# Five small edits to a fused attention and feed-forward kernel: a second load queue, a second buffer, a later transpose, another group order, smaller last stores

## The chip, the cores and the metric

The kernel runs on one core of one Trainium2 chip. The metric is device time in microseconds (us) of one execution. Before the change it was 820.72 us, the median of 3 runs (819.7 to 821.32). TensorE is written PE, VectorE DVE, ScalarE ACT, SyncE SP. A "q" after an engine's name means its sequencer issuing a DMA.

## The reference, cut to what matters

```python
# q, k, v: (8 batches, 8 heads, 576 tokens, 64); g_norm: (64,)
kv  = np.einsum('bhsd,bhse->bhde', k, v)
o   = np.einsum('bhsd,bhde->bhse', q, kv)
rms = np.sqrt(np.mean(o * o, axis=-1, keepdims=True) + 1e-06)
x   = (o / rms * g_norm)                  # then laid out as 4608 tokens x 512
a, b = x @ w1, x @ w2                     # 512 x 1024 each
out = ((a * b) @ w3) @ w_out              # 1024 x 1024, 1024 x 512
```

The four weights come as 64-bit floats, the rest in fp32.

## The kernel before

The 4608 tokens are worked on as 9 groups of 512. Each batch has 576 tokens, so 8 groups are the first 512 tokens of a batch, and the ninth, the *leftover group*, holds the last 64 tokens of all eight. The product w3·w_out is computed once, at the start (the *fold*), in 8 *chunks* of 128 columns of w3 and 128 rows of w_out. Each chunk is loaded as 64-bit words, converted to fp32 by two ACT and four DVE steps, transposed on PE and multiplied. PE's order is written by hand, and at the start that of ACT, DVE and SP too.

The loads of a chunk: the first one (i = 0) in four loads of 256 KB, the others in two of 512 KB, all from SP's queue. The first is converted in three pieces.

```python
src = w3[0:DF // 2, i * P:(i + 1) * P].rearrange("(m p) f -> p m f", p=P)
cols = w_out[i * P:(i + 1) * P, :].rearrange("p (c f) -> p c f", c=1)
n = 1 if i else 2
for h in range(n):
    load(slice(h * 512 // n, (h + 1) * 512 // n), src[:, h * 4 // n:(h + 1) * 4 // n, :])
for h in range(n):
    f = slice(h * DM // n, (h + 1) * DM // n)
    load(slice(512 + f.start, 512 + f.stop), cols[:, :, f])
# ... cut ...
cuts = [0, 1024] if i else [0, 256, 512, 1024]
```

The setup fills the four load buffers and then loads the norm's gain, 64 numbers, twice into a column of 128 partitions, from ACT's queue:

```python
for _ in range(RAW):                      # RAW = 4
    load_next()
nc.scalar.activation(const.tile([P, 1], FP32, name="warm"), eps_col, AF.Sqrt)
g_src = g_norm.rearrange("(d o) -> d o", o=1)
for e in range(2):
    nc.scalar.dma_start(out=g_col[e * D:(e + 1) * D, :], in_=g_src)
keep_warm(14)                             # filler matmuls
begin_next(); end_next()                  # convert chunk 0
turn_w3(0, 0)                             # transpose its w3 half
keep_warm(5)
# ... cut: for each chunk c: convert c + 1, multiply c, transpose c + 1 ...
```

The norm: ACT squares a bank of PSUM, DVE sums per head, with one buffer for the squares.

```python
for i in range(n):
    sq = work.tile([P, G], FP32, name="sq", bufs=1)[:, 0:w]
    nc.scalar.activation(sq, o_ps[i], AF.Square)
    nc.vector.tensor_reduce(out=inv[:, i], in_=sq.rearrange(...), axis=AX.X, op=ALU.add)
```

The attention of the next batch is cut into pieces, which run between the products of the present group. Every second batch also transposes the leftover tokens' q (`q_t_left`):

```python
pieces = [[(begin, 0, 1)], [(middle, 0)], [(turn, 0), (turn, 1)],
          [(begin, 2, 3)], [(middle, 1)], [(turn, 2), (turn, 3)], [], []]
if b % 2:
    pieces[0].append((q_t_left,))
```

The groups run in the order 0 to 8, the leftover group last; its results go out in eight stores of 128 KB from SP's queue:

```python
for m in range(2):
    for l in range(2):
        b = 2 * (2 * half + m) + l
        nc.sync.dma_start(out=out[b * S + G:(b + 1) * S, :],
                          in_=o_sbs[half][l * L:(l + 1) * L, m, :])
```

## Time and profile before

| of the profiled run, span 817.5 us | us |
|---|---|
| PE busy | 803.4 |
| PE waits for the identity matrix, at the start | 1.9 |
| PE waits for conversions at the start, two waits | 3.8 |
| PE waits at the leftover q's transposes | 1.1 |
| PE waits for normalised rows | 1.0 |
| from PE's last matmul to the end | 5.9 |

PE is busy for 98% of the span, so the time is PE's own work plus what PE waits for. Everything else matters only where it makes PE wait, at the start and at the end. The lines behind this table are in the prediction. Two further lines of before also belong here, and the prediction does not show them. The first is in the list of waits, on the row of PE's weight loads (columns: what waited, for what, us in total, times, longest); the second is in the full list of DMA issues (KB each, us from issue to landing).

```profile
PEld at L302 <- ACT kv_sb L284: 2.3, 4, 1.2
```

```profile
g_col<-in_g_norm_dram ACTq DMA_DIRECT2D x2, 0.2 KB, 3.8
```

The weight loads that feed PE waited 2.3 us in four places where the matmul row shows 1.1 us in two. And a load of 0.2 KB took 3.8 us to land.

### The profile page before, as it was taken

To read this page: it belongs to the slowest core of one execution; us is meant where nothing else is said; L and a number is where in the kernel's file an instruction comes from. 1 tells how busy PE (TensorE), PEld (TensorE's weight loads), DVE (VectorE), ACT (ScalarE), POOL (GpSimd) and SP (SyncE) were. 2 spreads that over 40 slices of the span, in tenths; PEclk is the share of its full clock that TensorE was granted. 3 is DMA by queue.
4 is the path that set the end of the run, shared out by engine and by line. 5 is a ranking of instruction groups with operands and counts; after the bars stand their busy time and mean duration, and the time that the engine had idled before them with its cause. 6 is when DMAs were issued, how large, how long until landed. Compare 5 with 4: busy or idle time off the path is not lost.

```text
span 817.5 us, 12566 instructions
## 1 busy us (share of the span) xinstructions
PE 803.4 (98%) x5334; PEld 675.4 (83%) x5334; DVE 364.7 (45%) x680; ACT 267.8 (33%) x499; POOL 1.8 (0%) x8
## 2 busy tenths in 40 slices
PE   7999999999999999999999999999999999999997
PEld 4455788888888888888888888888888888888886
DVE  6967997315521553155315531543154414512521
ACT  6677643234312331243123322331233212212210
POOL 0000000000000000000000000000000000000000
PEclk9999999999999999999999999999999999999999
DMA  9996434032103210312032202120210010001002
GB/s 315 331 334 173 147 91 91 1 128 62 32 1 128 71 36 1 105 58 57 1 104 71 59 1 85 61 76 1 89 41 1 1 52 1 0 1 52 1 0 52
DMA packets 60152, 59.53 MB, mean 73 GB/s; under 512 B 15425, under 2 KB 56385, under 8 KB 60097
## 3 DMA queue, kind: packets, MB, share of 16 engines
q1 hardware_dynamic: 59936, 58.73, 23.8%
q8 instruction: 42, 0.69, 0.4%
q14 instruction: 14, 0.11, 0.0%
q10 hardware_dynamic: 160, 0.00, 0.0%
HBM read 49.28 MB, written 9.44 MB: 72 GB/s over the span
## 4 chain that ended last, share of the span: by engine, by line
PE 93%; DVE 3%; ACT 1%; DMA 1%; issue 1%; SPq 0%; DVEq 0%; ACTq 0%
PE mm L470 78%; PE mm L455 5%; PE at L273 2%; PE at L343 2%; PE at L376 2%; PE at L292 2%; DMA raw<-in_moe_w_out_dram 1%; PE at L442 1%; DVE ab L149 1%; ACT kv_sb L284 0%; DVE w_sb L159 0%; DVE inv L312 0%; PE at L302 0%; PE at L361 0%; DVE w_sb L153 0%
## 5 line engine op out<-in xcount | busy, mean ns | idle before, releaser
L470 PE MATMUL mm<-xT,w_sb 128*128 128x256 f32 x768 | 176.2, 379 | 0.0
L470 PEld LDWEIGHTS mm<-xT,w_sb 128*128 128x128 f32 x768 | 145.9, 190 | 20.3 <-issue 0.5
L470 PE MATMUL mm<-xc,ws 128*128 128x256 f32 x576 | 130.2, 379 | 0.0
L470 PEld LDWEIGHTS mm<-xc,ws 128*128 128x128 f32 x576 | 109.4, 190 | 14.9
L483 ACT COPY u<-mm 128x512 f32<-128x512 f32 x90 | 52.7, 586 | 195.1 <-PE mm L470 194.4
L470 PE MATMUL mm<-w3o_sb,ab 128*128 128x256 f32 x432 | 96.2, 379 | 0.0
L596 DVE TENSOR_TENSOR c<-mm,u 128x512 f32<-128x512 f32 x36 | 24.9, 690 | 157.9 <-PE mm L470 157.7
L483 ACT COPY p<-mm 128x512 f32<-128x512 f32 x90 | 52.8, 586 | 129.8 <-PE mm L470 129.5
L470 PEld LDWEIGHTS mm<-w3o_sb,ab 128*128 128x128 f32 x432 | 82.1, 190 | 11.2
L470 PE MATMUL mm<-xc,w_sb 128*128 128x256 f32 x288 | 68.8, 382 | 0.0
L470 PE MATMUL mm<-raw 128*128 128x256 f32 x288 | 63.6, 379 | 0.0
L455 PE MATMUL mm<-chunks,ab 128*128 128x512 f32 x128 | 60.0, 601 | 1.9 <-DVE chunks L159 1.9
L470 PE MATMUL mm<-xT,ws 128*128 128x256 f32 x256 | 61.6, 383 | 0.0
L470 PEld LDWEIGHTS mm<-raw 128*128 128x128 f32 x288 | 54.7, 190 | 7.4
L470 PEld LDWEIGHTS mm<-xc,w_sb 128*128 128x128 f32 x288 | 52.8, 190 | 6.7
L312 DVE TENSOR_REDUCE inv<-sq 128x8 f32<-128x512 f32 (+1 forms) x40 | 25.2, 629 | 61.5 <-ACT sq L311 61.5
L470 PEld LDWEIGHTS mm<-xT,ws 128*128 128x128 f32 x256 | 46.7, 190 | 6.0
L625 DVE TENSOR_TENSOR raw<-mm,u 128x512 f32<-128x512 f32 x9 | 6.2, 692 | 97.0 <-PE mm L470 97.0
L597 DVE TENSOR_TENSOR ab<-c 128x256 f32<-128x256 f32 x108 | 45.7, 423 | 2.8
L455 PEld LDWEIGHTS mm<-chunks,ab 128*128 128x128 f32 x128 | 21.9, 190 | 23.5 <-issue 17.9
L596 DVE TENSOR_TENSOR c<-p,u 128x512 f32<-128x512 f32 x36 | 24.8, 689 | 27.3 <-ACT u L483 27.3
L311 ACT ACTIVATE sq<-at 128x512 f32<-128x512 f32 (+1 forms) x40 | 22.2, 555 | 41.1 <-PE at L343 21.7
(83 smaller groups left out, 779.2 us busy)
## 6 DMA issues: line engine op xcount, KB each, us to landing
raw<-in_moe_w_dram SPq DMA_DIRECT2D x31, 512.0 KB, 7.3
k_sb<-in_k_dram SPq DMA_DIRECT2D x32, 256.0 KB, 4.5
v_sb<-in_v_dram SPq DMA_DIRECT2D x32, 256.0 KB, 4.8
q_sb<-in_q_dram SPq DMA_DIRECT2D x32, 256.0 KB, 4.9
out_dram<-raw SPq DMA_DIRECT2D x16, 512.0 KB, 2.6
raw<-in_moe_w_out_dram SPq DMA_DIRECT2D x7, 512.0 KB, 8.2
kl_sb<-in_k_dram SPq DMA_DIRECT2D x8, 128.0 KB, 5.8
vl_sb<-in_v_dram SPq DMA_DIRECT2D x8, 128.0 KB, 5.5
```

What stands on the lines that cost most here:

```text
L149: nc.vector.scalar_tensor_tensor(out=low_bits, in0=hi, scalar=0x80000000, in1=low_bits, op0=ALU.bitwise_and, op1=ALU.bitwise_or,)
L273: nc.tensor.matmul(kv_ps[e * D:(e + 1) * D, r - rs[0], :], lhsT=k_sb[:, e, cols] if j < J else kl[:, 2 * r + e, :], rhs=v_sb[:, e, cols] i ...
L292: nc.tensor.transpose(qt_ps[:, e, i, :], q_sb[:, e, i * P:(i + 1) * P], ident)
L311: nc.scalar.activation(sq, o_ps[i], AF.Square)
L312: nc.vector.tensor_reduce(out=inv[:, i], in_=sq.rearrange("p (h d) -> p h d", d=D), axis=AX.X, op=ALU.add)
L343: nc.tensor.matmul(o_ps[l][tokens, n * D:(n + 1) * D], lhsT=qT[r][rows, e, i, tokens], rhs=kv_b[rows, e, r, :], start=True, stop=True,)
L376: nc.tensor.transpose(t_ps[:, j, :], st[r // 2][:, j // 2, j % 2, m:m + 2, :], ident)
L455: nc.tensor.matmul(sums_ps[half][m], lhsT=w3T[half, c][:, m, :], rhs=chunks[:, c, 1, :], start=(c == 0), stop=(c == KF - 1),)
L470: nc.tensor.matmul(ps[:, u, :], lhsT=lhsT(a_name, u, c), rhs=rhs(b_name, c),  start=(u == 0 and c == 0 and to is None), stop=(c == chunks ...
L483: nc.scalar.copy(t, ps)
L596: nc.vector.tensor_add(c, one, two)
L597: nc.vector.tensor_mul(dst, c[:, 0, :], c[:, 1, :])
```

## The change

The intent is to shorten the waits of the table. The first chunk is loaded from two queues and converted in parts of 512 columns; the squares get two buffers; the leftover q is transposed two pieces later; the leftover group becomes the last but one; and the last group is stored block by block.

```diff
-            n = 1 if i else 2
-            for h in range(n):
-                load(slice(h * 512 // n, (h + 1) * 512 // n), src[:, h * 4 // n:(h + 1) * 4 // n, :])
-            for h in range(n):
+            queues = (nc.sync,) if i else (nc.sync, nc.scalar)
+            n = len(queues)
+            for h, queue in enumerate(queues):
+                load(
+                    slice(h * 512 // n, (h + 1) * 512 // n),
+                    src[:, h * NH // n:(h + 1) * NH // n, :], queue,
+                )
+            for h, queue in enumerate(queues):
                 f = slice(h * DM // n, (h + 1) * DM // n)
-                load(slice(512 + f.start, 512 + f.stop), cols[:, :, f])
+                load(slice(512 + f.start, 512 + f.stop), cols[:, :, f], queue)
...
-        cuts = [0, 1024] if i else [0, 256, 512, 1024]
+        cuts = [0, 1024] if i else [0, 512, 1024]
...
-                sq = work.tile([P, G], FP32, name="sq", bufs=1)[:, 0:w]
+                sq = work.tile([P, G], FP32, name="sq")[:, 0:w]
...
-            pieces[0].append((q_t_left,))
+            pieces[2].insert(0, (q_t_left,))
...
+            if last:
+                rows = out[T * S:T * S + G, j * N:(j + 1) * N].rearrange("(p j) f -> p j f", j=J)
+                parts = ((0, 1), (1, 2)) if two is None else ((0, 2),)
+                for a, b in parts:
+                    if two is None:
+                        nc.scalar.copy(dst[:, a:b], one[:, a:b])
+                    else:
+                        nc.vector.tensor_add(dst, one, two)
+                    queue = nc.scalar if a else nc.sync
+                    queue.dma_start(out=rows[:, 2 * half + a:2 * half + b, :], in_=dst[:, a:b])
+                return
...
-    for T in range(NG):
-        pieces = iter(attention(T + 1) if T + 1 < B else [])
+    groups = [*range(B - 1), B, B - 1]
+    for n, T in enumerate(groups):
+        pieces = iter(attention(T + 1) if n + 2 < NG else [])
```

More of the change, by code (lines that the diff above doesn't have):

```diff
@@ L61 @@
     KF = DF // P
+    NH = KF // 2
     J = 4
@@ L179, in load_next, with load @@
         raw = raw_tile()
-        def load(where, src):
-            nc.sync.dma_start(out=raw[:, where].rearrange("p (c m) -> p c m", c=src.shape[1]), in_=src)
+        def load(where, src, queue=nc.sync):
+            queue.dma_start(out=raw[:, where].rearrange("p (c m) -> p c m", c=src.shape[1]), in_=src)
         if what == "w":
@@ L432, in attention @@
         return [steps(fs) for fs in pieces]
-    NH = KF // 2
     w3T = {}
@@ L603, in gates, with project @@
         )
-    def project(T, between=lambda: None):
+    def project(T, between=lambda: None, last=False):
         def store(half):
@@ L732 @@
                 run(sum_ab(p))
-        if T and T + 1 < NG:
-            run(combine_x(T + 1))
-        project(T, between if T == 0 else lambda: None)
+        last = n + 1 == NG
+        if T and not last:
+            run(combine_x(groups[n + 1]))
+        project(T, between if T == 0 else lambda: None, last)
         if T == 0:
```

## The prediction

> **What bounds the kernel now.** I read the page's totals first, to learn which engine leaves no room.
>
> ```profile
> span 817.5 us, 12566 instructions
> PE 803.4 (98%) x5334; PEld 675.4 (83%) x5334; DVE 364.7 (45%) x680; ACT 267.8 (33%) x499; POOL 1.8 (0%) x8
> ```
>
> TensorE (PE) is busy for 803.4 of 817.5 us, and the change removes none of its useful matmuls. So the whole prize lies in the 817.5 - 803.4 = 14.1 us in which PE stands still, plus such filler as stands in for waiting at the start. Next I asked what PE waited for (columns: engine and line, what ended the wait, us in total, times, longest).
>
> ```profile
> PE mm L254 <- POOL ident masks.py:199: 1.9, 1, 1.9
> PE mm L455 <- DVE chunks L159: 1.9, 1, 1.9
> PE at L442 <- DVE chunks L159: 1.9, 1, 1.9
> PE at L302 <- ACT kv_sb L284: 1.1, 2, 0.9
> PE at L376 <- DVE xn L321: 1.0, 4, 0.3
> ```
>
> These sum to 7.8 us. Another 5.9 us is the tail: the timeline shows PE's last matmul ending at 811.6. That leaves about 0.4 us of crumbs. The first wait, for the identity matrix, is untouched. The change aims at the other four and at the tail, so its ceiling is about 1.9 + 1.9 + 1.1 + 1.0 + 5.9 = 11.8 us, 1.4% of the time.
>
> For the start I followed the chain that ended last, in order of time (start, duration, what; links of 0.02 us left out).
>
> ```profile
> 3.36 6.68 DMA raw<-in_moe_w_out_dram
> ...
> 10.13 1.14 ACT ab L146
> ...
> 11.29 1.23 DVE ab L149
> 12.52 0.61 DVE chunks L153
> ...
> 13.15 0.70 DVE chunks L156
> ...
> 13.88 1.24 DVE chunks L159
> ...
> 15.16 0.66 PE at L442 x4
> 15.82 3.52 PE mm L455 x8
> ```
>
> From 15.16 on PE has no gap up to 48: a chunk takes it 3.52 + 0.44 = 3.96 us, and VectorE (DVE) converts one in 3.72 (its L159 steps start at 13.88, 17.61, 21.33). So what matters is when the conversion of the *second* chunk ends, at 15.11; all later work slides with it. That conversion starts when the second chunk's w_out lands, 6.68 us after its issue. The traffic of those microseconds, by windows (last two columns: share of the DMA engines' time, GB/s):
>
> ```profile
> 3.50:4.00 0.50, 0.50 (x4) 0.50 (x4) 0.00 (x0) 0.35 (x2) 0.00 (x0) 1.00 0.68 215
> 4.00:4.50 0.50, 0.50 (x5) 0.50 (x4) 0.38 (x2) 0.50 (x3) 0.00 (x0) 1.00 0.32 82
> 4.50:5.00 0.50, 0.50 (x4) 0.50 (x4) 0.47 (x3) 0.50 (x2) 0.00 (x0) 1.00 0.65 205
> 5.00:5.50 0.50, 0.50 (x5) 0.50 (x4) 0.47 (x3) 0.09 (x1) 0.00 (x0) 1.00 0.82 291
> ...
> 9.00:10.00 1.00, 0.00 (x0) 0.00 (x0) 0.93 (x3) 0.12 (x1) 0.00 (x0) 1.00 1.05 379
> ```
>
> There is a hole between 3.5 and 5.5 us: the first 512 KB of w3 is done and w_out, issued from 1.74 on, has barely begun. Afterwards the engines are full at about 380 GB/s.
>
> **What the Trainium skill says.** "DMA: Bandwidth & Descriptors", section "Issuing engines are not separate DMA queues": DMAs of all issuing engines share the same 16 DMA engines, and issuing from several saves only sequencer time. The trace agrees as far as it goes: six loads stand one after another in SyncE's queue from 0.74 to 3.8, about 0.5 us each, and once the engines are full no second queue could add anything. So I credit the second queue with the hole and the issue time, not with bandwidth. "Perfetto Trace Analysis", section "Optimization Strategy", says that repeating gaps on the engine that should be saturated can mean too few SBUF or PSUM buffers; the waits at L302 and L376 fit that (below). "DMA: Bandwidth & Descriptors", section "Anatomy of one DMA — SWDGE (gpsimd) path", puts a fixed cost of about 2.0 us on a DMA, mostly the write receipt; it speaks of the GpSimd path, but the small output stores here, on the SyncE queue, took 2.2 to 2.4 us to land. So the tail keeps that part whatever is done.
>
> **The change, part by part.**
>
> *First chunk from two queues, in parts of 512.* The four 256 KB loads of chunk 0 are issued two and two, so chunk 1's loads are issued two places earlier on SyncE: 2 x 0.55 = 1.1 us. Bytes decide how much of that arrives. Between 3.5 and 5.5 the engines moved (215 + 82 + 205 + 291) x 0.5 = 397 KB; at some 330 GB/s (the rate of the 3.0 to 3.5 window) they would have moved 660 KB. The missing 263 KB, at 380 GB/s, is 0.7 us. So chunk 1 lands 0.7 to 1.1 us earlier, at about 9.1. Its own conversion chain (5.0 us from landing to end) is unchanged. DVE must be free for it: chunk 0 now takes two conversions of 512 columns. The w3 half lands at about 4.0 in one piece; 0.67 + 0.69 + 0.42 + 0.43 + 0.69 (the 512-column durations of before) ends it near 7.0, about as the two 256-column conversions do (6.86). The w_out half lands about 1 us earlier than its 7.41 and ends near 9.3 instead of 10.33. So DVE is no obstacle and PE's steady stretch starts about 1.0 us earlier. Gain: **1.0 us**.
>
> *Two buffers for the squares* (in the diff, not in the title). One buffer made ScalarE wait for the first reduction before the second square. Timeline of the first normalisation:
>
> ```profile
> 60.17 0.60 ACT L311 ACTIVATE sq<-at 128x512 f32<-128x512 f32 x1 [1.32 <-PE at L343]
> 60.80 0.69 DVE L312 TENSOR_REDUCE inv<-sq 128x8 f32<-128x512 f32 x1 [4.91 <-ACT sq L311]
> 61.58 0.60 ACT L311 ACTIVATE sq<-at 128x512 f32<-128x512 f32 x1 [0.81 <-DVE inv L312]
> 62.21 0.69 DVE L312 TENSOR_REDUCE inv<-sq 128x8 f32<-128x512 f32 x1 [0.72 <-ACT sq L311]
> ```
>
> With two, the second square runs beside the first reduction and the second reduction starts near 61.5: 0.7 us earlier. PE's transposes of that result waited 0.28 + 0.21 us at 64.5 and 0.34 + 0.21 at 81.8; each pair is under 0.7. Gain: **1.0 us**. All later normalisations shorten as well, but PE does not wait there, so they give nothing.
>
> *Leftover q two steps later.* Its transposes come fourth in a piece that has three PSUM banks, so they wait until ScalarE has copied k-v out of the first:
>
> ```profile
> 107.31 0.66 PE L302 MATMUL at<-ident,ql_sb 128*128 128x128 f32 x4 [0.93 <-ACT kv_sb L284]
> ```
>
> Moved to the third piece, they take a bank long since read. The same 0.43 us of PE work is done elsewhere; the waits, 0.93 here and 0.15 at 260.4, go. The order of instructions shows the new place directly before the transposes of the normalised rows; those find their data at about 120.1 and 120.7, close to PE's new arrival, so up to 0.4 could come back, though DVE's order there now puts the normalisation ahead of weight sums; I leave that to the range. Gain: **1.1 us**.
>
> *Leftover group last but one.* Same matmuls, swapped order. Its rows (x_left) are finished in the group before its use, some 30 us of projection ahead, so nothing new is waited for. Gain by itself 0, but it lets the last stores be rows of a full batch.
>
> *Last group block by block.* Before, the end goes: last matmul 811.6, one ScalarE copy of 128x512 (0.58 us), then four stores from one queue at about 0.59 each, the last landing 2.4 us after its issue.
>
> ```profile
> 808.89 5.73 SPq L615 DMA_DIRECT2D out_dram<-raw  x8
> 811.62 0.58 ACT L623 COPY raw<-mm 128x512 f32<-128x512 f32 x1 [6.32 <-PE mm L470]
> ```
>
> The eight issues end at 814.62, so the last starts near 814.0 and lands at 816.4; the program then takes 1.1 us more. After: two copies of 128x256 (0.37 us each in the 128x256 copies of L592, some 0.7 together), each followed by one store on its own queue. The last store is issued about 0.8 us after the last matmul and lands 2.4 us later: 0.8 + 2.4 + 1.1 = 4.3 us of tail instead of 5.9. Three of the four issues, some 1.8 us, go, and the split copy costs 0.1 to 0.2 more. Gain: **1.6 us**.
>
> Sum: 1.0 + 1.0 + 1.1 + 1.6 = 4.7. 820.72 - 4.7 = **816.0 us**.
>
> **Rivals.** *(a) The start gives nothing:* the hole may be the latency of a first touch of w_out, not queueing, and two queues share the engines, so chunk 1 lands as late as before. For it: w_out came 2.4 us after issue, w3 about 1.1. Against: w_out is now issued 0.5 us or more earlier, so even a fixed latency shifts. Time: 817.0. *(b) The start gives much more:* if chunk 1's 6.68 us were mostly waiting behind the four loads and the order within one queue, it could land near 8.4, and DVE alone would set the start; its two 512 conversions end near 9.3 and chunk 1's four steps take 3.84, so 13.1 instead of 15.1: 2 us. Time: 815.0. *(c) DVE becomes the bound at 86 to 106:* it is busy 19.40 of 19.40 us there, and an earlier PE could run into its weight sums and give 1 to 2 us back. Against: the second gate's sums end at 97.6 and are used at 100.4, 2.8 us of slack, and DVE's own work moves forward with the start and the shorter normalisation. Time: 817.5.
>
> **Range and chances.** Single parts are uncertain by about 1 us at the start, 0.5 at each of the others, and the three runs of before spread over 1.6 us. That gives 813.8 to 818.2. To leave the 2% band the time would have to fall by 16.4 us, more than PE's whole idle time, or rise by as much, for which I see no mechanism: 0.01 and 0.01.
>
> **What would show it.** Right: PE's first long stretch begins near 14.2; the waits at L302 and L376 vanish; from the last matmul to the end about 4.3 us; PE's busy time nearly unchanged. Wrong: chunk 1's w_out still lands near 10.0; new waits of PE for DVE between 80 and 125 us; a last store that lands over 3 us after its issue; or a wait at the reordered groups after 640 us.

## The result, and the profile after

The changed kernel took 814.93 us, the median of 6 runs (813.25 to 817.62), against 820.82 us for the kernel before in the same rounds (6 runs, 819.7 to 821.32). The ratio is 0.9929, with a 95% interval of 0.991 to 0.9948: 0.7% less, and inside the predicted range. Here and below, a ratio is the mean time of one kernel's runs over that of the other's in the same rounds, so it is not quite the ratio of the medians quoted. Where I turn a ratio into microseconds, I multiply its distance from 1 by about 821.

The total hides what happened, so I start with the profile after: the page's totals, then PE's waits.

```profile
span 813.5 us, 12576 instructions
...
PE 804.1 (99%) x5334; PEld 676.2 (83%) x5334; DVE 363.5 (45%) x676; ACT 267.0 (33%) x498; POOL 1.8 (0%) x8
```

```profile
PE at L447 <- DVE chunks L160: 3.3, 2, 2.9
...
PE mm L460 <- DVE chunks L160: 0.4, 1, 0.4
```

The waits for the leftover q and for normalised rows are gone. The two at the start are not: together they were 3.8 us and are 3.7 (L442, L455 and L159 of before are L447, L460 and L160 here). And PE's busy time rose by 0.7 us with the same 5334 instructions, which is a first sign that something ran slower. The chain of waits at the start shows both (start us, duration us, what):

```profile
2.22 8.18 DMA raw<-in_moe_w_out_dram
...
14.25 1.24 DVE chunks L160
...
15.53 0.66 PE at L447 x4
16.19 5.13 PE mm L460 x8
```

The second chunk's w_out is issued 1.14 us earlier than before (2.22 instead of 3.36), but it takes 8.18 us instead of 6.68 and lands at 10.40 instead of 10.04. So PE's steady stretch begins at 15.53, not at 15.16 as before, and not at 14.2 as predicted. On top of it, its first eight matmuls take 5.13 us where they took 3.52. The windows tell both reasons (columns: window; length; busy us and instructions of PE, weight loads, DVE, ACT, POOL; granted clock; DMA share; GB/s):

```profile
6.00:7.00 1.00, 1.00 (x11) 1.00 (x10) 0.93 (x3) 1.00 (x2) 0.00 (x0) 1.00 0.69 192
7.00:8.00 1.00, 0.63 (x6) 0.44 (x6) 1.00 (x2) 0.24 (x1) 0.00 (x0) 1.00 0.74 216
8.00:9.00 1.00, 1.00 (x12) 1.00 (x10) 0.93 (x4) 0.59 (x1) 0.00 (x0) 1.00 0.72 245
...
16.00:17.00 1.00, 1.00 (x4) 0.40 (x3) 1.00 (x2) 0.78 (x2) 0.00 (x0) 0.56 1.10 396
17.00:18.00 1.00, 1.00 (x2) 0.49 (x2) 0.93 (x3) 1.00 (x2) 0.00 (x0) 0.50 1.00 373
18.00:19.00 1.00, 1.00 (x2) 0.34 (x1) 1.00 (x1) 0.91 (x1) 0.00 (x0) 0.50 1.15 371
```

First, the hole in the transfers, from 3.5 to 5.5 us before, has not been closed: it now lies between 6 and 9 us, at some 220 GB/s where the windows on either side have 350 and 361. Between 3.5 and 4.5, where by the rates before it w_out is first touched, the rate is now 367 and 311 GB/s. Second, the granted clock is half of full from about 16.1 to 19.5 us, just after PE stood still for 2.92 us in one piece. This is the 1.6 us by which the eight matmuls are longer.

The other three parts can be read at fixed places of the two traces. The two normalisations near the start, from PE's product to the end of its transposes, took 6.93 and 6.99 us (from 59.03 and 76.34) and take 6.11 and 6.17 (from 61.00 and 77.50): 0.82 + 0.82 = 1.6 us. The timeline of the first one after shows why; square and reduction now overlap, the pairs back to back:

```profile
62.14 1.09 ACT L317 ACTIVATE sq<-at 128x512 f32<-128x512 f32 x2 [1.32 <-PE at L349]
62.77 1.28 DVE L318 TENSOR_REDUCE inv<-sq 128x8 f32<-128x512 f32 x2 [4.91 <-ACT sq L317]
```

At the four leftover-q places the trace after gains on the one before by 1.15, 0.38, 0.38 and 0.36 us, each taken as the change in distance between like instructions ahead of and behind the place: 2.3 us together. At the end, PE's last matmul ends at 809.84 instead of 811.60, and the tail is 813.5 - 809.84 = 3.7 us instead of 5.9 (timeline, end of after):

```profile
809.87 0.65 ACT L633 COPY raw<-mm 128x256 f32<-128x256 f32 x2 [6.32 <-PE mm L475]
810.26 0.34 SPq L637 DMA_DIRECT2D out_dram<-raw  x1
810.54 0.36 ACTq L637 DMA_DIRECT2D out_dram<-raw  x1
```

| part | predicted gain | gain between the two profiled runs |
|---|---|---|
| start | 1.0 | -2.0 (0.4 later, 1.6 half clock) |
| squares | 1.0 | 1.6 |
| leftover q | 1.1 | 2.3 |
| order and stores at the end | 1.6 | 2.2 |
| sum | 4.7 | 4.1 |

The spans of the two profiled runs, 817.5 and 813.5, differ by 4.0 us; between 87 and 104 us some 0.2 us are given back. This is one pair of runs, and the profiled run of before, 819.27 us by the clock of the metric, is one of its faster ones; the means differ by 5.8 us. What the runs without a profile did cannot be read from a trace.

### The profile page after: what moved, and what is told of

It reads as the page before. It is cut to its first block, busy times and chain, and to the rows that moved or that the text cites. A ratio compares the mean times of both kernels' runs of the same rounds, so it can differ in the third digit from the quotient of the medians. Undisturbed runs are those within 1.5% of the kernel's fastest.

```text
span 813.5 us, 12576 instructions
## 1 busy us (share of the span) xinstructions
PE 804.1 (99%) x5334; PEld 676.2 (83%) x5334; DVE 363.5 (45%) x676; ACT 267.0 (33%) x498; POOL 1.8 (0%) x8
## 4 chain that ended last, share of the span: by engine, by line
PE 98%; DMA 1%; DVE 0%; ACT 0%; SPq 0%; issue 0%; ACTq 0%
PE mm L475 81%; PE mm L460 7%; PE at L279 3%; PE at L349 2%; PE at L298 2%; PE at L382 2%; DMA raw<-in_moe_w_out_dram 1%; PE at L447 1%; PE at L367 0%; PE at L391 0%; PE at L308 0%; SPq L183 0%; DVE chunks L160 0%; DVE ab L150 0%; ACT ab L147 0%; DVE chunks L157 0%
## 5 line engine op out<-in xcount | busy, mean ns | idle before, releaser
L488 ACT COPY u<-mm 128x512 f32<-128x512 f32 x90 | 52.8, 586 | 205.6 <-PE mm L475 185.5
L488 ACT COPY p<-mm 128x512 f32<-128x512 f32 x90 | 52.7, 586 | 134.3 <-PE mm L475 134.3
L460 PE MATMUL mm<-chunks,ab 128*128 128x512 f32 x128 | 61.6, 615 | 0.4 <-DVE chunks L160 0.4
L318 DVE TENSOR_REDUCE inv<-sq 128x8 f32<-128x512 f32 (+1 forms) x40 | 23.5, 626 | 58.4 <-ACT sq L317 58.4
L460 PEld LDWEIGHTS mm<-chunks,ab 128*128 128x128 f32 x128 | 22.5, 194 | 23.0 <-issue 17.4
L475 PE MATMUL mm<-w3o_sb,raw 128*128 128x256 f32 x144 | 32.6, 380 | 0.0
```

What stands on the lines that cost most here:

```text
L318: nc.vector.tensor_reduce(out=inv[:, i], in_=sq.rearrange("p (h d) -> p h d", d=D), axis=AX.X, op=ALU.add)
L460: nc.tensor.matmul(sums_ps[half][m], lhsT=w3T[half, c][:, m, :], rhs=chunks[:, c, 1, :], start=(c == 0), stop=(c == KF - 1),)
L475: nc.tensor.matmul(ps[:, u, :], lhsT=lhsT(a_name, u, c), rhs=rhs(b_name, c),  start=(u == 0 and c == 0 and to is None), stop=(c == chunks ...
L488: nc.scalar.copy(t, ps)
```

## The experiments

Twelve kernels ran in three jobs, all with the right result, each timed in 5 rounds beside the kernel before, which had medians of 820.8, 821.13 and 820.88 us (11 runs each). My theory was that the start costs about 2 us, from two causes, a moved hole in the transfers and a halved clock, and that the other three parts give more than predicted. The rivals: that the start is harmless and the gains elsewhere are simply as predicted, and, for the hole, that it comes from first touching w_out, from the limited number of DMA completion counters (SP's issue of the third chunk waits for an earlier landing until 4.60 us in the changed kernel), or from the tiny load of g_norm.

### The start alone, and all but the start

```diff
 # e1: the kernel before, plus the hunks with `queues` and `cuts`
 # e2: the changed kernel, with those two hunks undone
```

> Kernel before with the start of the change only (two queues, parts of 512). The prediction's step says 1.0 us faster than before (about 819.8), the second chunk's w_out landing near 9.1 and PE's long stretch starting near 14.2. My theory after seeing the trace of the changed kernel: no gain. The second chunk still lands near 10.4, the long stretch starts near 15.5, PE stands still for about 2.9 us before it and its clock may be halved for about 3.4 us after it, so 0.4 to 2 us slower than before (821 to 823).

> Changed kernel with the old start put back. If the start gains 1.0 us this is about 1 us slower than the changed kernel (815.9). If the start gains nothing or loses, as its trace says, this is as fast or up to 2 us faster than the changed kernel: 813 to 815, some 6.0 us under before (1.5 squares, 2.3 leftover q, 2.2 tail, all three read from the two traces).

The start alone took 823.01 us (821.32 to 824.16), ratio 1.002 (1.0004 to 1.0037): slower by about 1.6 us. Its trace repeats what the changed kernel showed: w_out lands at 10.55, PE starts at 15.66, the first eight matmuls take 5.13 us, and the clock is 0.50 between 18 and 20. So the first part of the change is a loss by itself, and no interplay with the others is needed for it.

All but the start took 814.03 us (812.93 to 815.16), ratio 0.9915 (0.9899 to 0.993), about 1.2 us better than the changed kernel by the ratios, although the two intervals overlap. That is less than the 2.0 us that the traces put on the start. Its trace shows where the rest went, in a wait that the prediction's third rival had placed elsewhere (timeline around 90 us; at the end of a line, the idle time before it and what ended it):

```profile
90.34 1.17 ACT L148 ACTIVATE w_sb<-raw 128x1024 f32<-128x1024 f32 x1 [1.26 <-DMA raw<-in_moe_w_dram]
91.40 0.58 ACT L484 COPY p<-mm 128x512 f32<-128x512 f32 x1
92.03 1.35 PE L471 MATMUL mm<-xT,ws 128*128 128x256 f32 x5 [0.91 <-ACT p L484]
```

ACT waits 1.26 us for a block of w1 and w2 to land, and in its order the copy of PE's product out of PSUM stands behind that block's conversion; so PE waits too, 1.5 us in two places. A PE that is earlier at 85 us runs into loads that are not.

### The tiny load moved away

```diff
-        g_src = g_norm.rearrange("(d o) -> d o", o=1)
-        for e in range(2):
-            nc.scalar.dma_start(out=g_col[e * D:(e + 1) * D, :], in_=g_src)
...
             elif c == 5:
                 load_pair(0, 1)
                 load_q_left(0)
+                g_src = g_norm.rearrange("(d o) -> d o", o=1)
+                for e in range(2):
+                    nc.scalar.dma_start(out=g_col[e * D:(e + 1) * D, :], in_=g_src)
```

> Changed kernel with the two loads of g_norm (64 elements of 4 bytes each) issued at the sixth chunk and not behind the first chunk. My theory: these tiny loads hold the stream back; their packets run through the very microseconds (6 to 9) in which the DMA engines moved only 150 to 260 GB/s. Then that hole goes, the second chunk lands near 9.2 and PE's long stretch starts near 14.3: 1.2 us faster than the changed kernel, 2.8 if the halved clock goes too (812 to 813.7). Rival: the hole comes from SyncE waiting for landings before it can issue the third chunk (2.72 to 4.60), or from one queue alone being too slow; then the hole stays at 6 to 9 and the time stays at 814.9.

This is the changed kernel with the loads of g_norm, two of 0.2 KB, issued at the sixth chunk instead of during the first. It took 812.24 us (812.08 to 812.84), ratio 0.9895 (0.9878 to 0.9912). The windows and the chain of this kernel:

```profile
6.00:7.00 1.00, 1.00 (x7) 1.00 (x7) 0.93 (x3) 1.00 (x2) 0.00 (x0) 1.00 1.13 401
7.00:8.00 1.00, 1.00 (x11) 1.00 (x11) 1.00 (x3) 0.17 (x1) 0.00 (x0) 1.00 0.99 390
8.00:9.00 1.00, 1.00 (x11) 1.00 (x10) 0.93 (x3) 0.84 (x2) 0.00 (x0) 1.00 1.07 360
```

```profile
13.79 0.66 PE at L447 x4
14.45 3.52 PE mm L460 x8
```

The hole is gone: 401, 390 and 360 GB/s in place of 192, 216 and 245. ACT starts the second chunk's conversion at 8.74 without any wait for a DMA, so its w_out had landed by then, at least 1.6 us earlier. PE's wait for it shrinks to 1.3 us, its stretch begins at 13.79, and the clock stays full. But the move also freed SP: its third chunk was issued from 2.76 on, and no longer after 4.60. So two explanations were left, the loads themselves or the completion counters they hold.

### Same counters, no scatter

```diff
-        g_src = g_norm.rearrange("(d o) -> d o", o=1)
         for e in range(2):
-            nc.scalar.dma_start(out=g_col[e * D:(e + 1) * D, :], in_=g_src)
+            nc.scalar.dma_start(
+                out=const.tile([1, D], FP32, name=f"g_row{e}"), in_=g_norm.rearrange("(o d) -> o d", o=1)
+            )
 # and the real loads at the sixth chunk, as above
```

> As e3 (loads of g_norm late), but two small loads of g_norm as one row of 256 bytes on one partition stand where they were, on the same queue and in the same order, so every load of the weights waits for the same completions as in the changed kernel (SyncE's third chunk still waits for the first landing). If the 64 elements of 4 bytes were what held the stream back, the hole at 6 to 9 us stays away and the time is that of e3 (812.2). If it was that the two loads take two of the eight completion counters, so that fewer weight loads are under way, the hole comes back and the time is that of the changed kernel (814.9).

Two loads of the same 256 bytes stand in the old place, but each goes to one partition as one row. SP's third chunk waits again (its w_out is issued at 4.94; 5.02 in the changed kernel, 3.25 with the loads moved). Yet there is no hole:

```profile
6.00:7.00 1.00, 1.00 (x6) 1.00 (x6) 0.93 (x3) 1.00 (x2) 0.00 (x0) 1.00 1.11 413
7.00:8.00 1.00, 1.00 (x10) 1.00 (x9) 1.00 (x3) 0.13 (x1) 0.00 (x0) 1.00 0.98 391
```

The time was 812.63 us (811.99 to 812.8), ratio 0.9896, as good as with the loads moved, and PE's stretch begins at 13.94. So neither the counters nor two loads of these bytes in this place make the hole. It is their form, the scatter of 64 single numbers over 64 partitions. In the trace of before, ACT's queue carries nothing else: 160 packets for 128 numbers. Those packets run from 2.6 to 6.0 us of the span before, and from about 5.6 to 9.7 us in the changed kernel, each time over the hole. By what means they slow the stream of the other queue is not shown by any run.

The scatter does not make such a hole everywhere. Issued at the sixth chunk, the same 160 packets run from 34.5 to 35.6 us in this kernel, and the rate stays up:

```profile
34.00:35.00 1.00, 1.00 (x7) 0.51 (x5) 0.96 (x2) 0.43 (x1) 0.00 (x0) 1.00 1.15 335
35.00:36.00 1.00, 1.00 (x3) 0.49 (x3) 0.97 (x1) 1.00 (x2) 0.00 (x0) 1.00 1.04 337
```

In the kernel of the section before, they run from 33.5 to 36.5 at 319, 305, 307 and 249 GB/s, and both kernels have windows as low as 207 to 247 just before, without them. What makes the start more sensitive was not tested.

### Without the second queue, the tiny load moved away

```diff
 # the changed kernel, with the hunks `queues` and `cuts` undone, and g_norm loaded at the sixth chunk
```

> Changed kernel with the old start and the late loads of g_norm: tells whether the second queue is worth anything once the tiny loads are out of the way. If yes, it is 0.5 to 1 us slower than e3 (812.7 to 813.2). If the engines are full either way, it is within 0.3 us of e3 (812.2), with PE's long stretch starting near 14.

It took 813.84 us (813.1 to 815.3), ratio 0.9915 (0.9893 to 0.9937). Its fastest run is slower than the slowest with two queues in the same job (812.8, the kernel with two rows), and the medians differ by 1.2 us. Two of its six runs, 814.93 and 815.3, have a mean granted clock of 0.998, which the control below reads as the half clock; the other four have a median of 813.5, still 0.8 us slower. The second queue, with its parts of 512, is therefore worth what the prediction gave it, about 1 us, but only once the scatter is out of its way. One thing stays open: on one queue the second chunk still lands at 10.05 although the rate between 4 and 5 us rose from 144 to 279 GB/s. It should have come earlier. More of the later chunks' bytes may have come among its own; no run separates that.

### Keeping PE busy in the gap

```diff
+            if c == 0:
+                keep_warm(12)
             turn_w3(...)
```

> Changed kernel with 12 filler matmuls on the identity (about 2.6 us) in the gap before the second chunk's transposes. My theory: the 2.9 us of standing still let the clock fall to half at 16 to 19.5 us, which cost 1.6 us; with the gap filled the clock column stays at 1.00 and the time falls by up to 1.6 us (to about 813.3), the long stretch still starting near 15.5. Rival: the clock falls for another reason (a fixed time after the start), then nothing changes: 814.9.

Twelve filler matmuls in the gap, in front of the second chunk's transposes; otherwise the changed kernel (chain of waits):

```profile
12.72 2.68 PE mm L260 x24
15.40 0.44 PE at L447 x4
15.84 3.52 PE mm L460 x8
```

With PE busy in the gap, the eight matmuls take 3.52 us again and the clock stays full. The time was 813.85 us (813.27 to 814.16), ratio 0.9912 (0.9896 to 0.9927), some 1.4 us better than the changed kernel by the ratios. That is near the 1.6 us of the trace. How much of the median the clock makes up is read with the control, next.

### The changed kernel again

> The changed kernel again, unaltered, as a control beside these runs: 813.2 to 815.5, ratio to before near 0.993.

No edit; it took 815.26 us (813.58 to 816.14), ratio 0.9928 (0.9909 to 0.9948). The hole is there again (231, 217 and 238 GB/s from 6 to 9) and w_out lands at 10.65, so that cause is steady. The half clock is not: PE stood still for 3.2 us in one piece, longer than in the first trace, and its clock stayed full:

```profile
15.77 0.66 PE at L447 x4
16.43 3.52 PE mm L460 x8
```

Nevertheless this run's span was 813.2, only 0.3 us better. What it had gained by the start, 1.4 us, had shrunk to 0.3 behind a wait of 1.0 us for ACT's copy (p, L488) in the stretch of 85 to 94 us, the same give-back as in all but the start. So in this run most of what a full clock gave was lost again at those loads.

The other runs say more about the median. The record has the mean granted clock of every run, and 3.4 us at half clock in 813 us lower it by 0.002. Of the twelve runs of the changed kernel, the six of the result and these six, eight have 0.998 (814.89 to 817.62 us, median 815.4) and four have 1.000 (813.25 to 815.0 us, median 813.5). The twenty runs of the filler kernel and of the three kernels without the hole on two queues, which all end in the same way, have 0.999 or 1.000. So two runs in three of the changed kernel had the half clock, and these were 1.9 us slower; without it the changed kernel is as fast as the kernel with the filler (813.85). The split is not as clean everywhere: in all but the start, the two runs with 0.997 (813.66 and 814.79) are no slower than the other four (812.93 to 815.16).

The traces also suggest why a gap of 2.92 us was followed by a half clock and one of 3.2 us was not. They list the moments at which the granted clock changed. It rose to full at 5.89 us and fell at 16.13 in the changed kernel, and rose at 6.36 and fell at 16.60 with the start alone: 10.24 us each time, three times the 3.41 us that the half clock then lasted. I count stretches of 3.41 us from the rise. In the last one before the fall PE stood still for 2.8 us in the changed kernel and 2.5 us with the start alone (whose gap was 3.19). In this control the clock had risen at 6.98, a stretch ended at 13.81 within the gap, and its two sides hold 1.2 and 2.0 us. With one queue and the tiny load moved away, the gap was 2.83 us in one piece, a stretch ended within it too, the longer side holds 1.6 us, and the clock stayed full. In no kernel whose clock stayed full does a stretch hold more than 2.0. That fits a limit between 2.0 and 2.5 us within stretches fixed in time; no edit tested it.

### The other parts one by one

```diff
 # e6: only this
-                sq = work.tile([P, G], FP32, name="sq", bufs=1)[:, 0:w]
+                sq = work.tile([P, G], FP32, name="sq")[:, 0:w]
 # e7: only this
-            pieces[0].append((q_t_left,))
+            pieces[2].insert(0, (q_t_left,))
 # e8: only `groups` and the stores of `last`
 # e9: only `groups`
```

> Kernel before with two buffers for the squares and nothing else. The prediction counts 1.0 us (the idle time that PE's records show at L376). The traces of before and changed show 0.8 and 0.7 us less between the product and the end of the transposes of each of the two normalisations, so I expect 1.5 us (about 819.3), PE's wait for xn gone from its list. A third possibility is that VectorE, full from 86 to 106 us, gives some of it back: then under 1.0.

> Kernel before with the leftover q's transposes moved and nothing else. The prediction counts 1.1 us from PE's matmul row. The weight-load row has 2.3 us in 4 visits for the same wait, and the two traces differ by 0.65 or more at the first and some 0.37 at each of the other three visits: I expect 2.0 to 2.3 us (818.6), the wait for kv_sb gone from PE's and from the weight load's list.

> Kernel before with the group order and the block stores and nothing else. The prediction counts 1.6 us; the changed kernel's trace has 3.7 us from the last matmul to the end where before has 5.9, so I expect 2.2 us (818.6), with a tail of 3.6 to 3.8 us.

> Kernel before with the group order only, the last group stored in two halves of 512 KB as every full group is. Tail worked out from before: copy 0.6, one issue 0.4 (counted in the landing), landing 2.6, end 0.9: about 4.2 to 4.5 us, so 1.4 to 1.7 of the tail's 2.2 us come from the order alone (819.2). Rival: the order only makes the block stores possible and gives nothing by itself (820.8).

| edit alone, on the kernel before | median us (range) | ratio (95%) | us by the ratio |
|---|---|---|---|
| start | 823.01 (821.32 to 824.16) | 1.0020 (1.0004 to 1.0037) | +1.6 |
| squares | 818.74 (817.89 to 819.79) | 0.9977 (0.9963 to 0.9992) | -1.9 |
| leftover q | 818.46 (817.92 to 820.66) | 0.9979 (0.9963 to 0.9995) | -1.7 |
| order and stores | 817.33 (817.24 to 818.92) | 0.9963 (0.9948 to 0.9978) | -3.0 |
| of it, order alone | 818.21 (817.92 to 819.55) | 0.9973 (0.9960 to 0.9987) | -2.2 |

The four edits sum to -5.0 us, the whole is -5.8; with about 1.3 us of uncertainty on each, they add up. Each trace agrees with its edit. With the squares alone, the wait for normalised rows is gone. With the leftover q alone, the wait for kv_sb is gone from the matmul row and the weight-load row alike, but 1.3 us of new waits for ACT's copies (p and u) appear, so the place where loads come just in time takes part of this gain back as well. With the order alone, the tail is 816.2 - 811.82 = 4.4 us; with the block stores too, 815.5 - 811.88 = 3.6 us. So most of the tail's gain, 1.5 us, is due to the order, as one large store takes the place of four small ones.

### A version that beats both

```diff
-        cuts = [0, 1024] if i else [0, 512, 1024]
+        cuts = [0, 1024] if i > 1 else [0, 512, 1024]
 # and g_norm loaded at the sixth chunk, as above
```

> e3 with the second chunk converted in two parts of 512 too, so that its transposes can begin after the w3 half. The transposes then start about 1 us earlier (12.7), but VectorE needs 3.72 us for each further chunk and PE 3.96, so the third chunk's conversion holds PE again: at most 0.2 us better than e3 (812.0 to 812.3).

It took 812.16 us (811.88 to 812.51), ratio 0.9892 (0.9872 to 0.9913). Beside the changed kernel in the same job (815.26) it is 0.4% faster, with no overlap of the runs, and 1.1% under the kernel before. The conversion of the second chunk in two parts adds nothing that I can tell from noise: moving the tiny loads alone gave 812.24. The start's chain in this kernel runs through the third chunk's w_out, issued at 3.24 and landed at 11.99, so the bound had moved on.

## Why the prediction was right or wrong

The total, 816.0 predicted and 814.93 measured, was right, and it was right by cancellation, which is luck: one step had the wrong sign, and three were too small.

**Start: wrong.** The step that failed is "So chunk 1 lands 0.7 to 1.1 us earlier, at about 9.1", with its "Gain: 1.0 us". It landed at 10.40. I took the hole for idle time that an earlier issue would fill, and never asked what caused it. The hole belonged to the scattered loads of g_norm on ACT's queue, which in the changed kernel come after that queue's two large loads, and the hole moved with them, from 3.5 to 5.5 us to 6 to 9, right among the second chunk's bytes. The trace of before had the evidence, 0.2 KB in 3.8 us in the list of DMA issues and 160 packets without bytes to speak of on ACT's queue, and I did not read it. Rival (a), a slow first touch of w_out, named the right outcome for a wrong reason: the first touch at 3.5 to 4.5 us ran at 311 to 367 GB/s. With the loads moved, PE started at 13.79, a little better than the 14.2 of the prediction. So its number came out near, but its premise, that the earlier issue alone fills the hole, did not hold. The half clock was not foreseen: in the trace of before, PE's idle time at the start lay in two pieces of 1.9 us; the changed kernel put most of it in one, and two runs in three then had the half clock. The prediction's own test, "chunk 1's w_out still lands near 10.0", was the one that struck.

**Squares: right mechanism, too small.** The term was 1.0 us, read from PE's idle time; the distance from product to transposes shrank by 1.6. A transpose's record lasts 0.27 us and more, while packed ones start 0.11 us apart and overlap; where waits pull them apart, part of the waiting therefore counts as busy.

**Leftover q: right mechanism, too small.** The term was "0.93 here and 0.15", 1.1 us from the matmul row. The offsets of the two traces give 2.3. The weight-load row had 2.3 in four places, and it is the better witness here. The 0.4 us that I feared would come back did not, at this place.

**Order: wrong attribution.** "Gain by itself 0" counted only PE; alone, the order took 1.5 us off the tail. The sum for the tail did contain it.

**Tail: right, slightly small.** 4.3 us predicted, 3.7 measured: the last store was issued 0.7 us after the last matmul (predicted 0.8), landed in 2.1 (2.4), and the program ended 0.9 later (1.1).

**Rival (c): partly real, in another place.** Some of an earlier PE is given back, from 0 to 1.5 us depending on kernel and run. It does not happen in DVE's weight sums at 97 to 100 us but at 87 to 92, where blocks of w1 and w2 land late and ACT's copies stand behind their conversion.

## What to carry to other kernels

Before you fill a hole in the transfers, find out which packets run in it; a load of 256 bytes that scatters single numbers over partitions can cost the main stream more than a microsecond (here w_out landed at least 1.6 us later), and here it was enough to issue it later. Measure what a wait costs as the change in distance between two fixed instructions, or on the weight-load row, and not only by PE's idle time. When a total comes out right, check each term by itself, as errors of opposite sign hide one another. Read the mean granted clock of each run beside its time before you explain a median.

## What the Trainium skill lacked or had wrong

- "DMA: Bandwidth & Descriptors", section "Rules for kernel authors", says that a non-contiguous last dimension becomes one descriptor per element. The case here is next to it, as the last dimension is a single number, and the trace agrees: 160 packets of 4 bytes for 128 numbers, the other 32 being 16 to a load, as the 256 KB loads on the same queue have them too. The page has no figure for what such a load costs the stream of another queue. Here two of 0.2 KB went with a fall from some 380 to some 220 GB/s for about 3 us, as rows of 256 bytes they did not, and at the sixth chunk of that kernel the scattered ones passed at 335 GB/s.
- "TensorE: Matmul & The Clock Gate", section "Part 1: The HAM clock gate (the "warmup" mystery)", has the clock halve after at least one idle window of about 3.4 us, by windows that run freely, and warns of gaps above that. The half clock lasted 3.4 us, as it says of the way back, but it followed a gap of only 2.92 us in the changed kernel, and a gap of 3.2 us in another run of it had none. Counted in stretches of 3.41 us from the rise of the clock, 2.8 and 2.5 us of standing still were enough and 2.0 were not. So a gap below the limit is not safe.
- "Perfetto Trace Analysis", section "Identifying the Most-Contended Engine", warns that pipelined PE instructions look smaller in the trace. It does not say that PE's idle time by the matmul row also understates a wait. Here that row had 1.1 us, the weight-load row 2.3, and removing the wait was worth 2.3 by the two traces (1.7, give or take 1.3, by the times of that edit alone).
- The prediction leaned on "DMA: Bandwidth & Descriptors", section "Issuing engines are not separate DMA queues", by which a second issuing engine saves issue time only. The runs are near that, but not at it: the second chunk's w_out was issued 1.0 us earlier with two queues (2.21 instead of 3.20), PE's stretch began 1.4 us earlier (13.79 instead of 15.18), and the median fell by 1.2. What the rest is was not tested.
